# Joining the weights over the first two batches, with batch 0 in two visits, in a fused attention and MLP kernel

## The chip, the cores and the metric

The kernel runs on one core of one Trainium2 chip. The metric is the device time of one execution in microseconds (us). Three timed executions of the kernel before took 1055.58, 1061.92 and 1061.16 us, a median of 1061.16 us. A further execution was profiled.

## What is computed

A clustered attention feeds a mixing MLP. There are 4 batches, 8 heads, 768 positions and a head width of 64.

```python
q_assign = np.argmax(np.einsum('bhsd,hcd->bhsc', q_n, c_n), axis=-1)
k_assign = np.argmax(np.einsum('bhsd,hcd->bhsc', k_n, c_n), axis=-1)
mask = q_assign[:, :, :, None] == k_assign[:, :, None, :]
scores = np.where(mask, scale * np.matmul(q, k.transpose(0, 1, 3, 2)), -1000000000.0)
attn = softmax over the last axis
x = np.matmul(attn, v), heads side by side: (4, 768, 512)

h = x.transpose(0, 2, 1) @ U @ V          # mixing over the positions, rank 32
u = x + h.transpose(0, 2, 1)
out = u + np.maximum(u @ w_ch1, 0.0) @ w_ch2   # 512 -> 2048 -> 512
```

The weights of the MLP and of the mixing arrive as 64-bit floating-point numbers, seen as 64-bit integers.

## The kernel before

**Attention.** The 8 heads of a batch are taken in pairs, so there are 16 steps `i` ("head pairs"), four to a batch. A step loads queries and keys (`load`, tile `R`), rounds them to the upper part on ScalarE (`split_hi`, L390), subtracts for the lower part (`split_lo`, L395), assigns clusters, and places everything in rows of a large tile `arena` by DMA from the SP queue (`copy_rows`, L225; `place_clusters` copies the tile `ohT` there in four DMAs). `rowmax` multiplies keys by queries on TensorE (L455) and takes row maxima on VectorE (L457). `scores` (L493, L495) multiplies again with the maxima subtracted; ScalarE takes the exponential (L498, tile `pr`); GpSimd adds the tiles `pr` for the row sums (`weights`, L508); `values` multiplies by v (L516), ScalarE copies the result out (L520, twice in a step, once for each half). After the last step of a batch, `mix_u`, `mix_sum` and `mix_v` form `u`, and one DMA of 1536 KB writes it to memory (`u_scr`, L581).

**MLP.** `w_ch1` and `w_ch2` are cut into 8 tiles `k` of 256 hidden columns. A pair is one batch with one tile k; there are 32 pairs, in the order batch 0 with k 0 to 7, then batch 1, and so on. A pair makes seven products (a Strassen-like scheme: `product`, 42 matmuls, L687 to L689), into two buffers of PSUM named `ps_h`. The products' operands are sums of quarters of `u` (`split_u`, L633 and L634, seven a batch) and of a weight tile (`add_w` on GpSimd, L653, `split_w`, L660 and L662). VectorE combines the products (L697), ScalarE copies the first (L701, once a pair), takes the relu (L730), VectorE its lower part (`hl`, L727), and `gemm2` multiplies by the tile of `w_ch2` (36 matmuls, L740 to L742, operand split by `split_w2`, L671 on ScalarE and L669 on GpSimd). A batch's results stay in six accumulators `y` of PSUM until its last pair, where `finish` adds `u` (L749) and stores. The lower halves of a weight tile are subtracted on GpSimd in the first eight pairs and on VectorE afterwards (`split_w`).

**Joining.** A weight is turned from 64 to 32 bits in the kernel: half a tile (128 x 512) is loaded (`in_w`, 512 KB), ScalarE scales the upper words (L179), and three VectorE operations build the result (`join`, L189, L190, L192), which a DMA writes to `w_scr` (256 KB, L211). There are 32 half tiles. The first `EARLY` = 16 are joined during the attention, one every `PACE` = 6.5 units of the plan, with an intermediate in PSUM (`ps_t`). The other 16 come `LATE` = 1.985 units apart from the start of the MLP on, with the intermediate in SBUF (`rw_b`). Each tile is read again from `w_scr` when a pair uses it (`fetch_w`).

**Order.** Every step is put on one list with a planned time, by the tables `times`, `mixes`, `stages`, `mlp`, `order0` and `spots`. The list is sorted, and its order is the order of the instructions on each engine and in each queue; an engine waits at an instruction whose inputs aren't there. A step of the attention is 12 units of planned time, a pair of the MLP 7. `M0` is the unit at which the MLP starts. Planned times set order only, never a time of day.

**Where operands lie.** `operand` gives the 7 operand tiles of a batch places out of 9 in `arena`, in rotation, so two places of the next batch are free while a batch runs, and the others come free product by product in its last pair.

Of the kernel before, what the change touches and what calls it, by code (L numbers as in the profile page):

```python
# [45 lines left out]
P = 128  # L46
# [12 lines left out]
    "load0":          (-34.72, -34.25, -43.39,   None,   None,  -24.6),  # L59
    "load1":          (-26.03, -29.07, -30.74,   None,   None, -23.361),  # L60
    "sims":           ( -25.1, -28.59, -28.44,   None,   None, -21.52),
    "clusters_T":     (-19.416, -19.005, -18.681,   None, -13.278,  -13.9),
    "place_clusters": (-18.532, -16.49, -15.63,   None, -11.358, -12.11),
    "split_hi0":      (-29.17, -30.23, -24.29,   None,   None, -20.71),
    "split_lo0":      (-24.63, -24.44, -24.29,   None,   None, -18.43),
    "split_hi1":      (-23.89, -23.584, -24.34,   None,   None, -19.53),
# [876 lines left out]
```

## Time and profile before

| | |
|---|---|
| median of the timed executions | 1061.16 us |
| the profiled execution's own time | 1058.02 us |
| its span, first to last instruction | 1056.2 us |
| mean granted TensorE clock | 0.979 |
| busy: TensorE, VectorE, ScalarE, GpSimd | 93%, 67%, 42%, 56% |
| first product of the first pair | 503.4 us |

The attention fills the first 503 us of the span, the MLP the rest. A busy share is a mean over both; the prediction reads each part by itself. In rows of the timeline the first column is the start, the second the length, both in us; what stands in square brackets is how long the engine sat idle before that instruction, and what released it.

### The profile page before, as it was taken

The numbers are of one execution on the slowest core, as the hardware profiler recorded it, in microseconds if no ns is written. First come the engines' busy times: TensorE is split into PE (matmuls) and PEld (weight loads), VectorE is DVE, ScalarE is ACT, GpSimd is POOL, SyncE is SP. The second block draws the span as 40 slices with busy tenths as digits, with TensorE's granted clock in tenths as the row PEclk, the third lists the DMA queues.
The fourth block names the chain that finished last, engine by engine and source line by source line (L and its number), as shares of the span: only waits on it lengthen the run. The fifth ranks groups of instructions, "written<-read, shape, count | busy, mean of one in ns | idle before, by whom it ended". The sixth has DMA issues, their size and how long they took to land.

```text
span 1056.2 us, 14186 instructions
## 1 busy us (share of the span) xinstructions
PE 986.9 (93%) x5227; PEld 766.5 (73%) x5227; DVE 703.6 (67%) x1114; ACT 446.4 (42%) x633; POOL 590.3 (56%) x410
## 2 busy tenths in 40 slices
PE   6999999789998999998898898999999999999998
PEld 4666665565655676664677787888878888788887
DVE  5698777566876776646489867655486554865554
ACT  4454554345544556465233344223342234422321
POOL 4466676558756879766555667344373443734420
PEclk8899999899999999999999998999999999999999
DMA  6664564756547574600256751422115222152121
GB/s 164 172 149 121 145 173 102 232 143 162 162 106 225 157 190 107 200 1 25 99 183 204 240 195 44 169 79 101 70 71 178 80 102 70 71 179 76 44 101 60
DMA packets 43658, 135.99 MB, mean 129 GB/s; under 512 B 6539, under 2 KB 11141, under 8 KB 43077
## 3 DMA queue, kind: packets, MB, share of 16 engines
q1 hardware_dynamic: 43216, 135.00, 42.4%
q8 instruction: 41, 0.67, 0.3%
q14 instruction: 29, 0.23, 0.1%
q10 hardware_dynamic: 372, 0.10, 0.0%
HBM read 82.84 MB, written 20.97 MB: 98 GB/s over the span
## 4 chain that ended last, share of the span: by engine, by line
PE 62%; DVE 18%; DMA 7%; issue 4%; ACT 3%; POOL 3%; SPq 1%; ACTq 0%; DVEq 0%; POOLq 0%
PE o_ps L516 9%; PE y L741 6%; PE y L742 6%; PE y L740 6%; PE ps_h L687 6%; PE ps_h L688 6%; PE ps_h L689 6%; PE ps_max L455 5%; DMA rw<-in_w 4%; PE st L493 4%; PE st L495 4%; DVE m L457 3%; DVE arena L634 2%; DVE rw_t L192 2%; DVE hl L727 2%
## 5 line engine op out<-in xcount | busy, mean ns | idle before, releaser
L457 DVE TENSOR_REDUCE m<-ps_max 128x1 f32<-128x384 f32 x384 | 195.3, 548 | 108.9 <-PE ps_max L455 107.3
L508 POOL TENSOR_TENSOR T<-T,pr 128x768 f32<-128x768 f32 x120 | 227.8, 1898 | 60.3 <-ACT pr L498 36.5
L498 ACT ACTIVATE pr<-st 128x768 f32<-128x768 f32 x192 | 154.8, 811 | 84.2 <-PE st L495 68.9
L687 PE MATMUL ps_h<-arena,combos 128*128 128x384 f32 x448 | 154.2, 344 | 15.6 <-DVE c L697 15.0
L730 ACT ACTIVATE hh<-c 128x768 fp32r<-128x768 f32 x64 | 54.2, 846 | 243.6 <-DVE c L697 243.6
L742 PE MATMUL y<-w,hl 128*128 128x512 f32 x384 | 153.0, 399 | 1.8 <-DVE hl L727 1.7
L741 PE MATMUL y<-w,hh 128*128 128x512 f32 x384 | 153.9, 401 | 0.0
L740 PE MATMUL y<-w,hh 128*128 128x512 f32 x384 | 152.5, 397 | 0.0
L688 PE MATMUL ps_h<-arena,combos 128*128 128x384 f32 x448 | 151.5, 338 | 0.0
L689 PE MATMUL ps_h<-arena,combos 128*128 128x384 f32 x448 | 151.2, 338 | 0.0
L455 PE MATMUL ps_max<-arena 128*128 128x384 f32 x384 | 127.6, 385 | 19.8 <-DMA arena<-arena 4.3
L653 POOL TENSOR_TENSOR sums_w<-rw 128x256 f32<-128x256 f32 x64 | 52.6, 842 | 156.8 <-DVE combos L660 126.2
L516 PE MATMUL o_ps<-pr,vt 128*64 128x384 f32 x768 | 131.8, 492 | 6.8 <-ACT pr L498 6.0
L669 POOL TENSOR_TENSOR w<-w2f,w 128x1024 fp32r<-128x1024 f32 x32 | 78.3, 2447 | 77.3 <-ACT w L671 74.1
L455 PEld LDWEIGHTS ps_max<-arena 128*128 128x128 f32 x384 | 70.8, 196 | 60.7 <-issue 23.7
L727 DVE SCALAR_TENSOR_TENSOR hl<-c,hh 128x768 fp32r<-128x768 f32 x64 | 76.3, 1193 | 52.4 <-ACT hh L730 52.4
L493 PE MATMUL st<-arena 128*128 128x384 f32 x384 | 107.9, 363 | 0.9 <-ACT pr L498 0.7
L687 PEld LDWEIGHTS ps_h<-arena,combos 128*128 128x128 f32 x448 | 84.9, 190 | 32.5 <-DVE c L697 18.6
L508 POOL TENSOR_TENSOR T<-pr 128x768 f32<-128x768 f32 x30 | 57.0, 1899 | 87.0 <-ACT pr L498 86.8
L516 PEld LDWEIGHTS o_ps<-pr,vt 128*64 128x64 f32 x768 | 52.3, 137 | 73.1 <-issue 61.7
L495 PE MATMUL st<-arena 97*128 97x384 f32 x384 | 101.1, 345 | 1.4 <-DMA arena<-mT 1.4
L688 PEld LDWEIGHTS ps_h<-arena,combos 128*128 128x128 f32 x448 | 85.0, 190 | 7.6
(123 smaller groups left out, 1542.5 us busy)
## 6 DMA issues: line engine op xcount, KB each, us to landing
rw<-in_w SPq DMA_DIRECT2D x32, 512.0 KB
rw<-w_scr SPq DMA_DIRECT2D x32, 512.0 KB
w2f<-w_scr SPq DMA_DIRECT2D x32, 512.0 KB
R<-in_qk SPq DMA_DIRECT2D x32, 384.0 KB
arena<-arena SPq DMA_DIRECT2D x32, 384.0 KB
arena<-arena SPq DMA_DIRECT2D x64, 192.0 KB
u<-u_scr SPq DMA_DIRECT2D x16, 768.0 KB
w_scr<-rw_t SPq DMA_DIRECT2D x32, 256.0 KB
```

Source lines behind the costliest of these rows:

```text
L455: nc.tensor.matmul(ps[:, 0:HS], x1[:, 0, g // 2, g % 2, t * P:(t + 1) * P], x1[:, 1, h, g % 2, :], start=True, stop=True)
L457: nc.vector.reduce_max(live["m2", i][:, h, u:u + 1], ps[:, 0:HS], axis=AX.X)
L493: nc.tensor.matmul(st[:, j, 0:HS], x1[:, 1, hk, j, ks], x1[:, 0, h, j, :], start=True, stop=False)
L498: nc.scalar.activation(pr, st[:, :, 0:HS], AF.Exp, scale=SCALE)
L508: eng.tensor_add(T, live["p", i, h, 0] if c == 1 else T, live["p", i, h, c])
L516: nc.tensor.matmul(o_ps[64 * j:64 * j + 64, 0:HS], vv[:, c, j, :], pr[:, j, :], start=(c == 0), stop=(c == NT - 1))
L687: nc.tensor.matmul(ps, ah[:, d], oh[:, d], start=(d == 0), stop=False)
L688: nc.tensor.matmul(ps, ah[:, d], ol[:, d], start=False, stop=False)
L689: nc.tensor.matmul(ps, al[:, d], oh[:, d], start=False, stop=(d == 1))
L740: nc.tensor.matmul(y, hh[:, f, ts], w2[:, 0, f, :], start=(k == 0 and f == 0), stop=False)
L741: nc.tensor.matmul(y, hh[:, f, ts], w2[:, 1, f, :], start=False, stop=False)
L742: nc.tensor.matmul(y, hl[:, f, ts], w2[:, 0, f, :], start=False, stop=(k == NK - 1 and f == 1))
```

## The change

It has three parts.

1. **Joining spread.** 12 half tiles are joined during the attention, 9.53 units apart. The other 20 are joined in the first two batches of the MLP at the times in a new table `joins`, each relative to M0, by a new function `convert`: twelve of them build the weight tile in the place where its pair reads it, and write it to memory for later batches; eight (`STAGED`, half tiles 16 to 23) go through a tile `joined` to `w_scr`, as before. Each stage of `convert` (load, scale, join, store) has its offset in the row `late` of `stages`. The join's intermediate is the result tile itself, in SBUF. The sequence of the tiles (`blocks`) is written out.
2. **Another order of the pairs.** `runs` sets batch 0 with k 0 to 3, batch 1 with k 0 to 7, batch 0 with k 4 to 7, batch 2, batch 3. After the first visit `finish` adds the partial result to `u` and stores it to `u_scr`, from which the second visit fetches it. Batch 0 and batch 1 both keep their operands, in 14 places: 12 in `arena`, 2 in a new tile. Batch 1's operands are made in the pairs 2 to 4 (counted from 0), where they were made in the pairs 6 and 7. A second buffer `w2f_odd` takes the odd tiles of `w_ch2`. The lower halves of weight tiles are subtracted on GpSimd up to the pair 12.
3. **All tables of planned times are new**, with a table `lead` for the first six score tiles of step 0 and `paces` for the row maxima of the first steps.

```diff
 stages = {
-    "mix":  (  4.41,   7.02,  11.43,  15.04,  16.45,  17.16),
-    "w":    (36.161, 38.329, 40.954,  43.05),
-    "late": ( 9.201,   10.9,   11.5,   12.3),
+    "mix":  ( 4.442,  9.237, 21.481, 15.135, 28.889,  17.93),
+    "w":    ( 30.85, 37.709, 40.748, 43.339),
+    "late": ( -4.02, -1.242, -0.505,  0.183),
 }
-PACE, LATE, EARLY = 6.5, 1.985, 16
+PACE, EARLY = 9.53, 12
+STAGED = (16, 24)
+joins = [ 12.42, 18.256, 17.874, 23.279, 21.865, 30.275, 36.483, 42.327, 44.241, 48.068, 50.38, 53.5, 57.087, 57.953, 63.136, 62.997, 68.029, 70.82, 72.995, 78.476]
...
-    "place_clusters": (-18.532, -16.49, -15.63,   None, -11.358, -12.11),
+    "place_clusters": (-16.663, -19.154, -20.524,   None, -13.79, -13.047),
-    "rowmax":         (-14.88, -14.94,  -14.8, -12.18, -7.978, -10.78),
+    "rowmax":         (-14.783, -15.801, -17.043, -10.988, -8.892, -11.482),
...
+    runs = ((0, 0, 4), (1, 0, 8), (0, 4, 8), (2, 0, 8), (3, 0, 8))
+    pairs = [(r, b, k) for r, (b, k0, k1) in enumerate(runs) for k in range(k0, k1)]
...
     def operand(b, o):
-        s = (7 * b + order.index(o)) % 9
-        at = 0 if s == 8 else 2 * XS + 2 * HB * s
+        s = order.index(o) + (7 if b in (1, 2) else 0)
+        if s < 12:
+            at = 2 * HB * ((s + 4) % 12)
+            x = arena[:, at:at + 2 * HB]
+        else:
+            x = live["operands"][:, s - 12]
...
+    def convert(s, stage):
+        (k, m), half = blocks[s // 2], s % 2
+        cols = slice(512 * half, 512 * half + 512)
+        rw, g, joined = live["late_w"]
+        rw, g = rw[:, half], g[:, half]
+        direct = not STAGED[0] <= s < STAGED[1]
+        if stage == 0:
+            if half == 0 and direct:
+                live["f", k, m] = weight_tile(k, m)
+            nc.sync.dma_start(out=rw, in_=w[k, m, :, cols])
+        elif stage == 1:
+            nc.scalar.mul(g, words(rw)[1], 2.0 ** -112)
+        elif stage == 2:
+            t = (live["f", k, m][:, cols] if direct else joined).bitcast(I32)
+            merge(rw, g.bitcast(I32), t, t)
+        elif not direct:
+            nc.sync.dma_start(out=w_scr[k][m][:, cols], in_=joined)
+            stored.add((k, m, half))
+        elif half:
+            nc.sync.dma_start(out=w_scr[k][m], in_=live["f", k, m])
+            stored.update({(k, m, 0), (k, m, 1)})
...
-    def finish(b, j):
+    def finish(g, j):
+        r, b, k = pairs[g]
         h, t = divmod(j, HT)
-        u, y = live["u", b, h], live.pop(("y", b, j))
+        u, y = live["u", b, h], live.pop(("y", r, j))
         nc.vector.tensor_add(u[:, t, :], y, u[:, t, :])
-        nc.sync.dma_start(out=out[b, j * P:(j + 1) * P, :], in_=u[:, t, :])
+        if k == NK - 1:
+            nc.sync.dma_start(out=out[b, j * P:(j + 1) * P, :], in_=u[:, t, :])
+        elif t == HT - 1:
+            nc.sync.dma_start(out=u_scr[b][:, h * HT:(h + 1) * HT, :], in_=u)
...
-    for s in range(4 * NK):
+    for s in range(EARLY):
         for stage in range(4):
-            at(stages["w"][stage] + PACE * s if s < EARLY else M0 + stages["late"][stage] + LATE * (s - EARLY),
-               load_weights, s, stage)
+            at(stages["w"][stage] + PACE * s, load_weights, s, stage)
+    for s in range(EARLY, 4 * NK):
+        for stage in range(4):
+            at(M0 + joins[s - EARLY] + stages["late"][stage], convert, s, stage)
...
-            at(m + step, split_w, g, k // 2, k % 2 == 1)
+            at(m + step, split_w, pairs[g][2], nc.gpsimd if g < 13 else nc.vector, k // 2, k % 2 == 1)
```

Three places show how the order moves. The first is the SP queue around the store of batch 0's `u` (`u_scr`). Before:

```order
L581 DMA u_scr_102<-xt 128x3072
L171 DMA rw<-in_w 128x512
L211 DMA w_scr_1_87<-rw_t 128x512
L225 DMA arena<-arena 32x1536 x2
L225 DMA arena<-ohT 32x2x384 x4
```

Now (`L593` is the store, `L177` a load of half a weight tile):

```order
L177 DMA rw<-in_w 128x512
L237 DMA arena<-arena 64x1536 x2
L593 DMA u_scr_102<-xt 128x3072
L223 DMA w_scr_0_88<-rw_t 128x512
L237 DMA arena<-ohT 32x2x384 x4
L237 DMA arena<-arena 32x1536 x4
L347 DMA R<-in_qk 128x768 x2
L177 DMA rw<-in_w 128x512
```

The weight load that stood right behind the store stands eleven DMAs behind it, and the load ahead of the store has two copies between itself and the store.

The second place is VectorE in the joining part of the MLP, before in the pair 4 (`rw_b` and `rw_t` by L189 to L192 are joins, L697 combines products, L727 is the relu's lower part):

```order
L189 TENSOR_SCALAR rw_b<-rw_g 128x512
L190 SCALAR_TENSOR_TENSOR rw_b<-rw_g,rw_b 128x512
L192 SCALAR_TENSOR_TENSOR rw_t<-rw,rw_b 128x512
L697 TENSOR_TENSOR c_5718<-rw_t,ps_h 128x384
L727 SCALAR_TENSOR_TENSOR hl<-c_5718,hh 128x768
L697 TENSOR_TENSOR rw_t<-ps_h,rw_g 128x384
L697 TENSOR_TENSOR c_5810<-ps_h,rw_t 128x384
L189 TENSOR_SCALAR rw_b<-rw_g 128x512
L190 SCALAR_TENSOR_TENSOR rw_b<-rw_g,rw_b 128x512
L192 SCALAR_TENSOR_TENSOR rw_t<-rw,rw_b 128x512
L697 TENSOR_TENSOR c_5810<-ps_h,rw_t 128x384
```

Now, in the pairs 4 and 5 (`joined` by L194 to L197 is a join, L745 combines, L775 is the relu's lower part):

```order
L194 TENSOR_SCALAR joined<-late_g 128x512
L195 SCALAR_TENSOR_TENSOR joined<-late_g,joined 128x512
L197 SCALAR_TENSOR_TENSOR joined<-late_rw,joined 128x512
L745 TENSOR_TENSOR c_5820<-ps_h,rw_g 128x384
L745 TENSOR_TENSOR rw_g<-ps_h,rw_g 128x384
L745 TENSOR_TENSOR rw_t<-ps_h,rw_g 128x384
L745 TENSOR_TENSOR c_5820<-rw_t,ps_h 128x384
L775 SCALAR_TENSOR_TENSOR hl<-c_5820,hh 128x768
L745 TENSOR_TENSOR rw_t<-ps_h,rw_g 128x384
L745 TENSOR_TENSOR c_5898<-ps_h,rw_t 128x384 x2
```

Before, a join stood after every two or three combinations; now seven combinations and a lower part pass between this join and the next.

The third place is VectorE where batch 1's operands are made, in the pairs 3 and 4 (L686 is `split_u`, L798 is `finish`):

```order
L686 TENSOR_TENSOR arena<-turned,arena 128x768 x2
L775 SCALAR_TENSOR_TENSOR hl<-c_5618,hh 128x768
L798 TENSOR_TENSOR u<-y_5223,u 128x512
L745 TENSOR_TENSOR c_5678<-ps_h,rw_g 128x384
L798 TENSOR_TENSOR u<-y_5249,u 128x512
L686 TENSOR_TENSOR operands<-turned,operands 128x768
L194 TENSOR_SCALAR joined<-late_g 128x512
L195 SCALAR_TENSOR_TENSOR joined<-late_g,joined 128x512
L197 SCALAR_TENSOR_TENSOR joined<-late_rw,joined 128x512
L745 TENSOR_TENSOR rw_g<-ps_h,rw_g 128x384
```

Before, the same place (the pairs 6 and 7, `split_u` at L634) held no joins, and the six additions of `finish` followed it:

```order
L634 TENSOR_TENSOR arena<-turned,arena 128x768 x2
L697 TENSOR_TENSOR c_6201<-ps_h,rw_g 128x384
L634 TENSOR_TENSOR arena<-turned,arena 128x768
L697 TENSOR_TENSOR rw_g<-ps_h,rw_g 128x384
L660 TENSOR_TENSOR combos_107<-rw,combos_107 128x768
L634 TENSOR_TENSOR arena<-turned,arena 128x768
```

A batch's operands, the six additions and joins now meet in the same two pairs.

More of the change, by code (lines that the diff above doesn't have):

```diff
@@ L172, in fetch, with words, merge @@
         return rw
+    def words(rw):
+        w = rw.bitcast(I32).rearrange("p (n two) -> p n two", two=2)
+        return w[:, :, 0], w[:, :, 1].bitcast(F32)
     def upper(rw):
         r, n = rw.shape
-        g = home[0].tile([P, 512], F32, name="rw_g")[0:r, 0:n]
-        high = rw.bitcast(I32).rearrange("p (n two) -> p n two", two=2)[:, :, 1].bitcast(F32)
-        nc.scalar.mul(g, high, 2.0 ** -112)
-        return rw, g.bitcast(I32), None
-    def join(rw, g, t):
-        r, n = rw.shape
-        low = rw.bitcast(I32).rearrange("p (n two) -> p n two", two=2)[:, :, 0]
-        t = home[0].tile([P, 512], I32, name="rw_t")[0:r, 0:n]
-        b = (work("ps_t").bitcast(I32) if home[0] is raw else home[0].tile([P, 512], I32, name="rw_b"))[0:r, 0:n]
+        g = raw.tile([P, 512], F32, name="rw_g")[0:r, 0:n]
+        nc.scalar.mul(g, words(rw)[1], 2.0 ** -112)
+        return rw, g.bitcast(I32)
+    def merge(rw, g, b, t):
         nc.vector.tensor_scalar(b, g, 3, None, op0=ALU.logical_shift_left)
@@ L191, in join @@
                                        op0=ALU.bitwise_and, op1=ALU.bitwise_or)
-        nc.vector.scalar_tensor_tensor(out=t, in0=low, scalar=29, in1=b,
+        nc.vector.scalar_tensor_tensor(out=t, in0=words(rw)[0], scalar=29, in1=b,
                                        op0=ALU.logical_shift_right, op1=ALU.bitwise_or)
-        return rw, g, t
+    def join(rw, g):
+        r, n = rw.shape
+        t = raw.tile([P, 512], I32, name="rw_t")[0:r, 0:n]
+        merge(rw, g, work("ps_t").bitcast(I32)[0:r, 0:n], t)
+        return t.bitcast(F32)
     parts, stored = {}, set()
-    blocks = sorted(((k, m) for k in range(NK) for m in range(2)), key=lambda x: (x[0] + x[1], -x[1]))
+    blocks = ((0, 0), (1, 0), (0, 1), (2, 0), (1, 1), (3, 0), (2, 1), (3, 1),
+              (4, 0), (5, 0), (4, 1), (5, 1), (6, 0), (7, 0), (6, 1), (7, 1))
     def load_weights(s, stage):
@@ L678, in product @@
     def product(g, p):
-        b, k = divmod(g, NK)
+        _, b, k = pairs[g]
         a, o = products[p]
@@ L814, in clustered_attention_moe @@
             h, c = divmod(k, NT)
[L815 removed]
+            at(when("scores", i) + (lead[k] if i == 0 and k < GV else k), scores, i, h, c)
             at(when("values", i) + GV * (k // GV) + GV - 1 + 0.001 * (k % GV), values, i, h, c)
@@ L860, in splits, with fetches @@
             at(m + step, fn, *args)
-    ng = B * NK
-    at(t_w0, fetch_w, 0, 0)
+    def fetches(time, g, m):
+        k = pairs[g][2]
+        s = 2 * blocks.index((k, m))
+        if s < EARLY or STAGED[0] <= s < STAGED[1] or any(x[2] == k for x in pairs[:g]):
+            at(time, fetch_w, k, m)
+    ng = len(pairs)
+    fetches(t_w0, 0, 0)
     weights_of(0, t_sums)
-    at(t_w1, fetch_w, 1, 0)
-    at(t_w2, fetch_w, 0, 1)
+    fetches(t_w1, 1, 0)
+    fetches(t_w2, 0, 1)
     for h in range(2):
@@ L874, in clustered_attention_moe @@
     for g in range(ng):
-        b, k = divmod(g, NK)
+        r, b, k = pairs[g]
         m = M0 + 7 * g
```

176 lines of the change are left out of this document (91 added, 85 removed).

## The prediction

> **What bounds the kernel now.** I read the page first: the busy shares, then the strip of 40 slices.
>
> ```profile
> PE 986.9 (93%) x5227; PEld 766.5 (73%) x5227; DVE 703.6 (67%) x1114; ACT 446.4 (42%) x633; POOL 590.3 (56%) x410
> PE   6999999789998999998898898999999999999998
> PEclk8899999899999999999999998999999999999999
> ```
>
> TensorE is the bound, and the change takes none of its matmuls away. A gain can only come from its idle time and from stretches at a lower granted clock. Next came the windows of the two stages (columns: length; busy us of TensorE, of its weight loads, VectorE, ScalarE, GpSimd; clock; DMA share; GB/s).
>
> ```profile
> 503.00:1056.00 553.00, 530.00 (x2601) 463.06 (x2597) 349.16 (x440) 190.30 (x254) 251.27 (x182) 0.99 0.33 115
> 0.00:503.00 503.00, 456.85 (x2630) 303.47 (x2630) 354.44 (x674) 256.06 (x379) 339.02 (x229) 0.97 0.54 144
> ```
>
> The attention leaves 503 - 457 = 46 us idle and loses about 3% of 503 = 15 us to the clock. The MLP leaves 23 us and loses about 5. Both are spread, so I looked for repeated work that should take equal times.
>
> In the attention, ScalarE copies the result of each half step. These are the ends of steps 2, 10, 11 and 12.
>
> ```profile
> 125.89 0.48 ACT L520 COPY os<-o_ps 128x384 f32<-128x384 f32 x1 [3.16 <-PE o_ps L516]
> ...
> 369.61 0.48 ACT L520 COPY os<-o_ps 128x384 f32<-128x384 f32 x1 [2.79 <-PE o_ps L516]
> ...
> 394.12 0.48 ACT L520 COPY os<-o_ps 128x384 f32<-128x384 f32 x1 [2.86 <-PE o_ps L516]
> ...
> 423.44 0.48 ACT L520 COPY os<-o_ps 128x384 f32<-128x384 f32 x1 [2.55 <-PE o_ps L516]
> ```
>
> Step 11 took 24.5 us, step 12, with the mixing of a batch inside, 29.3. Neither holds a join. Steps 3 to 10, six plain and two with mixing, would take 6 x 24.5 + 2 x 29.3 = 205.6 us at that pace; they took 243.7. So 38 us are lost where the joins are.
>
> In the MLP, ScalarE copies the first product once a pair. These are pairs 1, 8, 9, 14 and 16.
>
> ```profile
> 519.97 0.48 ACT L701 COPY rw_g<-ps_h 128x384 f32<-128x384 f32 x1 [1.87 <-PE ps_h L689]
> ...
> 657.39 0.48 ACT L701 COPY rw_g<-ps_h 128x384 f32<-128x384 f32 x1 [0.65 <-PE ps_h L689]
> 673.06 0.48 ACT L701 COPY rw_g<-ps_h 128x384 f32<-128x384 f32 x1 [0.77 <-PE ps_h L689]
> ...
> 751.35 0.48 ACT L701 COPY rw_g<-ps_h 128x384 f32<-128x384 f32 x1 [1.00 <-PE ps_h L689]
> ...
> 789.71 0.46 ACT L701 COPY rw_g<-ps_h 128x384 f32<-128x384 f32 x1
> ```
>
> A clean pair takes 15.67 us. A switch of batches without joins (pairs 14 to 16) costs 38.36 - 2 x 15.67 = 7.0 us over that. From pair 1 to pair 8 it is 137.4 us for seven pairs and one switch: 137.4 - 109.7 - 7.0 = 20.7 us are lost while 16 joins run.
>
> **The change, part by part.** The sum is made against the profiled execution's 1058.0 us (span 1056.2); it lies 3.1 us under the median of 1061.2.
>
> *1. The hole behind the store of batch 0's u.*
>
> ```profile
> 183.91 1.78 SPq L581 DMA_DIRECT2D u_scr<-xt  x1
> 185.75 0.43 SPq L171 DMA_DIRECT2D rw<-in_w  x1
> 197.28 0.66 ACT L179 ACTIVATE rw_g<-rw 128x512 f32<-128x512 f32 x1 [10.19 <-DMA rw<-in_w]
> 190.00:195.00 5.00, 3.59 (x22) 1.35 (x20) 1.02 (x2) 0.00 (x0) 2.10 (x2) 1.00 0.96 362
> 195.00:200.00 5.00, 0.43 (x2) 0.30 (x4) 0.00 (x0) 2.72 (x4) 0.34 (x1) 0.88 0.05 12
> 200.00:205.00 5.00, 5.00 (x17) 3.86 (x14) 3.15 (x6) 2.24 (x4) 1.51 (x2) 0.50 0.81 186
> ```
>
> The weight load is queued right behind 1536 KB. ScalarE stands at the join's scaling for 10.2 us with exponentials behind it, TensorE idles 1.41 + 4.57 = 6.0 us and then runs 5 us at half clock, 2.5 us more. The change issues each weight load 6.86 units ahead of its scaling (37.709 - 30.85), where it was 2.17; at 24.5 / 12 = 2.04 us a unit that is 14 us against 4.4, and the order shows this load ahead of the store. I take -8 us, between -9 and 0 (another load in the same place). What could be late next is the copies of `ohT`, which now come two places behind the store.
>
> *2. Four joins fewer in the attention.*
>
> ```profile
> L190 DVE SCALAR_TENSOR_TENSOR ps_t<-rw_g,ps_t 128x512 int32<-128x512 int32 (+2 forms) x19 | 12.6, 664 | 0.7
> L192 DVE SCALAR_TENSOR_TENSOR rw_t<-rw,ps_t 128x512 int32<-128x512 int32 (+2 forms) x19 | 12.4, 655 | 0.7
> L189 DVE TENSOR_SCALAR ps_t<-rw_g 128x512 int32<-128x512 int32 (+2 forms) x19 | 12.4, 652 | 0.0
> ```
>
> One costs VectorE 0.65 + 0.66 + 0.66 = 1.97 us and holds one of four PSUM buffers. Four make 7.9 us. VectorE isn't full in this stage (354 of 503), so not all of it is on the path: between 0 and -8, I take -3, nearer to the end where it hides. The 12 that stay are also further apart (9.53 units against 6.5); that is in item 3.
>
> *3. The other tables of the attention.* Of the 38 us, items 1 and 2 take 11; 27 are left in steps 3 to 10, and the start and the end have holes of their own. A table's worth can't be read from its numbers. The longer leads speak for a gain: `load0` of a usual step stands 11.1 units ahead of its rounding (-40.53, -29.39), where it was 5.6. One lead is shorter (the second rival). I take -5, between -25 and +15.
>
> *4. Joins thinned in the MLP.*
>
> ```profile
> L189 DVE TENSOR_SCALAR rw_b<-rw_g 128x512 int32<-128x512 int32 x16 | 14.8, 925 | 1.9 <-ACT rw_g L179 1.7
> L190 DVE SCALAR_TENSOR_TENSOR rw_b<-rw_g,rw_b 128x512 int32<-128x512 int32 x16 | 15.9, 996 | 0.5
> L192 DVE SCALAR_TENSOR_TENSOR rw_t<-rw,rw_b 128x512 int32<-128x512 int32 x16 | 18.5, 1159 | 0.5
> L727 DVE SCALAR_TENSOR_TENSOR hl<-c,hh 128x768 fp32r<-128x768 f32 x12 | 18.4, 1531 | 6.4 <-ACT hh L730 6.4
> L697 DVE TENSOR_TENSOR rw_t<-ps_h,rw_g 128x384 f32<-128x384 f32 x11 | 6.1, 552 | 3.1 <-PE ps_h L689 2.9
> ```
>
> Here a join costs 3.08 us. A pair without joins needs 2 x 1.53 + 7 x 0.55 = 6.9 us of VectorE. In pairs 2 to 6 the order has 3 joins a pair: 6.9 + 9.2 = 16.1 of 15.67 us, more than there is, and TensorE must wait. In the new order pairs 5 to 10 have 2 or 3, mostly 2: 13.1 of 15.67. Pair 2 has four (19.2 us), so some 4 us stay there. Thirteen joins' worth of lesser collisions at perhaps 0.4 us make 5 more; that is an estimate between nothing and the 1.3 us a join that the 20.7 us show now. So 9 to 10 of the 20.7 us stay: -11, between -21 and +5.
>
> *5. Batch 1's operands among the joins.* Seven subtractions and six additions of `finish` in the pairs 3 and 4:
>
> ```profile
> L634 DVE TENSOR_TENSOR arena<-turned,arena 128x768 fp32r<-128x768 f32 x28 | 42.1, 1512 | 13.0 <-ACT arena L633 12.9
> L749 DVE TENSOR_TENSOR u<-y,u 128x512 f32<-128x512 f32 x24 | 16.4, 686 | 5.9 <-PE y L742 5.9
> ```
>
> 7 x 1.51 + 6 x 0.69 = 14.7 us beside 2 x 6.9 and two joins, 6.2: 34.7 us in two pairs and a switch, 31.3 + 7.0. It fits barely. At pairs 6 and 7 the same work without joins already made a hole (640 to 645, below). I take +2, between 0 and +6.
>
> *6. One more switch of batches.* Pair 12 needs no new operands. Six additions, 4.1 us of VectorE, go beside pairs that have no joins any more; two stores and two loads go on the SP queue. +1, between 0 and +3.
>
> *7. The later switches.* Seven of 14 places are free for the next batch, where two of nine were. Of the 7.0 us, 24 transposes are work (some 4 us); the rest is waiting. Twice -1: -2, between -5 and 0.
>
> Sum: -8 - 3 - 5 - 11 + 2 + 1 - 2 = -26. From 1058.0 that is 1032, from the median 1035; I say 1033.
>
> A rule weighs against items 4 and 5, and these rows show its effect.
>
> ```profile
> 548.31 0.42 DVE L189 TENSOR_SCALAR rw_b<-rw_g 128x512 int32<-128x512 int32 x1
> 555.43 2.41 DVE L189 TENSOR_SCALAR rw_b<-rw_g 128x512 int32<-128x512 int32 x1
> 555.18 2.39 POOL L660 TENSOR_TENSOR combos<-sums_w,combos 128x1024 fp32r<-128x1024 f32 x1 [3.48 <-ACT combos L662]
> 555.00:560.00 5.00, 1.91 (x10) 1.36 (x8) 4.93 (x6) 0.10 (x1) 3.84 (x3) 1.00 0.46 173
> 560.00:565.00 5.00, 4.66 (x16) 4.19 (x17) 4.00 (x6) 2.48 (x5) 1.82 (x3) 0.66 0.81 262
> ```
>
> The same operation took 0.42 us, and 2.41 while a GpSimd operation ran; it ended 0.3 us after that one, and TensorE idled 3.1 us and then had clock 0.66. The Trainium skill ("SBUF — State Buffer", Who interferes with whom) says that the two engines share a port pair that one holds for a whole instruction while the other is blocked. The trace agrees. By that rule alone the three operations of a join could each wait out one GpSimd operation. The change keeps GpSimd at its subtractions for the pairs 8 to 12 too, so all 20 joins run beside it. That gives the first rival.
>
> **The rivals.**
>
> *Joins as dear as now.* If what a join costs TensorE is its wait for GpSimd and not the crowding, 20 joins cost 20 x 1.3 = 26 us instead of the 10 in my sum: +16, 1048. For it: the row at 555.43. Against: in the window 535 to 640 VectorE's joins stand so close that any delay lands on a product.
>
> *Cluster rows late.* In a usual step (nine of sixteen) `place_clusters` stands at -16.66 and the first row maximum at -14.78 + 0.39: 2.3 units or 4.6 us, where it was 3.9 units or 8.0.
>
> ```profile
> 434.87 2.69 SPq L225 DMA_DIRECT2D arena<-ohT  x4
> 436.95 5.85 DMA arena<-ohT
> 640.00:645.00 5.00, 1.97 (x7) 1.54 (x6) 3.72 (x5) 3.98 (x5) 4.92 (x4) 0.76 0.01 3
> ```
>
> From the first issue to the landing it took 436.95 + 5.85 - 434.87 = 7.9 us. Covered before by 8.0, it would be short by 3.3 us in nine steps, and a hole of that size brings a lower clock (0.66 after 3.1 us idle), 1.7 us each: 9 x 5.0 = 45, so 1077, slower. It decides if the SP queue reaches these copies only at their planned place. Against it: the queue runs ahead of the other engines where nothing holds it, and the tile copied is made no later than before. The Trainium skill ("TensorE: Matmul & The Clock Gate", Part 1) puts the clock's window at about 3.4 us; by it such a hole could also cost nothing more than itself. That would be 9 x 3.3 = 30 us and 1062.
>
> *The tables find most of the 27 us.* Item 3 at -25 gives 1012. For it: step 11 shows that a step can run in 24.5 us. Against: that step holds no join, and twelve joins stay.
>
> That the change doesn't thin the joins can be left out: the order shows it.
>
> **How the numbers follow.** My forecast, items near their chosen values, has a chance of 0.60, with 1018 to 1045 as its own range. Joins as dear as now: 0.18. Most of the 27 us found: 0.10. Cluster rows late, in whole or in good part: 0.12. A range of 1008 to 1056 holds the first and nearly all of the next two, and leaves out the late cluster rows and some tail, about 0.17. One per cent, which is about what can be told from no change here, puts the bounds at 1050.5 and 1071.8. Faster: 0.60, 0.10, and of the dear joins 0.08, together 0.78. Within 1%: 0.10 of the dear joins and 0.02 of late rows, 0.12. Slower: 0.10.
>
> **What would show it.** Item 1: no ScalarE wait of 10 us for `in_w`, and no slice at 0.5 clock near 200 us. Items 2 and 3: the first product starts at about 488 us instead of 503 or 504. Item 4: pairs 5 to 11 at 16 to 16.5 us. Item 5: a hole in pairs 2 to 4. The first rival would show in pairs of 17 us or more up to pair 11; the second in waits of `rowmax` for `ohT`. I am wrong if the attention is longer than 503 us, or the first half of the MLP isn't shorter.

## The result, and the profile after

The changed kernel takes 1031.1 us (median of 4 runs, 1029.85 to 1033.91) beside 1059.45 us of the kernel before on the same chip (4 runs). The ratio is 0.974 with a 95% interval of 0.970 to 0.978. 1033 us were forecast. The profiled execution is the longest of the four, 1033.9 us with a span of 1032.1; the span before was 1056.2, so 24.1 us went.

The page of the changed kernel, busy shares and two lines of the strip of 40 slices (25.8 us each):

```profile
PE 979.0 (95%) x5227; PEld 764.5 (74%) x5227; DVE 715.4 (69%) x1110; ACT 443.1 (43%) x633; POOL 622.8 (60%) x420
...
PE   7999999999999999989978999899989999899998
PEclk8999999999999999999998999999999999999999
```

The low slices in the middle are now the one from 439 us on, lightly, and those from 516 to 568 us: pairs 2 to 4 of the MLP.

Its windows, the MLP from 470 us on and the attention ahead of it (length; TensorE, weight loads, VectorE, ScalarE, GpSimd; clock; DMA share; GB/s):

```profile
470.00:1032.00 562.00, 530.57 (x2607) 463.99 (x2605) 363.22 (x449) 191.27 (x259) 282.90 (x192) 0.99 0.34 119
0.00:470.00 470.00, 448.40 (x2623) 300.50 (x2623) 352.16 (x662) 251.87 (x374) 339.87 (x228) 0.99 0.54 147
```

The attention is 33 us shorter: its idle time on TensorE fell from 46 to 21.6 us, and TensorE's busy time from 456.9 to 448.4, at a granted clock of 0.99 instead of 0.97. The MLP became longer, 562 us instead of 553, with 31.4 us idle instead of 23. So the total is where the forecast put it, and its parts are not.

ScalarE's copies at the ends of steps 2, 10, 11 and 12, to set beside those of before:

```profile
121.62 0.48 ACT L532 COPY os<-o_ps 128x384 f32<-128x384 f32 x1 [3.16 <-PE o_ps L528]
...
339.15 0.48 ACT L532 COPY os<-o_ps 128x384 f32<-128x384 f32 x1 [3.53 <-PE o_ps L528]
...
364.73 0.48 ACT L532 COPY os<-o_ps 128x384 f32<-128x384 f32 x1 [3.58 <-PE o_ps L528]
...
394.54 0.48 ACT L532 COPY os<-o_ps 128x384 f32<-128x384 f32 x1 [4.15 <-PE o_ps L528]
```

Steps 3 to 10 take 339.15 - 121.62 = 217.5 us, where they took 243.7; step 11 takes 25.6 and step 12 29.8, about as long as before (24.5 and 29.3). The gain lies in the steps with the joins, as it should if the loss of 38 us there was real. The windows of these eight steps, before and now, show what went:

```profile
125.89:369.61 243.72, 221.35 (x1272) 146.18 (x1273) 174.36 (x335) 122.90 (x178) 164.14 (x88) 0.97 0.59 162
121.62:339.15 217.53, 212.88 (x1275) 142.86 (x1276) 166.70 (x323) 119.90 (x174) 166.49 (x90) 1.00 0.60 167
```

TensorE's idle time fell from 22.4 to 4.7 us, and its busy time by 8.5 us at the higher clock.

The copies of the first product of pairs 0, 1, 3, 4, 5, 6, 11 and 31 in the MLP:

```profile
471.31 0.48 ACT L749 COPY rw_g<-ps_h 128x384 f32<-128x384 f32 x1 [0.75 <-PE ps_h L737]
...
490.98 0.48 ACT L749 COPY rw_g<-ps_h 128x384 f32<-128x384 f32 x1 [4.16 <-PE ps_h L737]
...
527.41 0.46 ACT L749 COPY rw_g<-ps_h 128x384 f32<-128x384 f32 x1
550.59 0.47 ACT L749 COPY rw_g<-ps_h 128x384 f32<-128x384 f32 x1
573.21 0.48 ACT L749 COPY rw_g<-ps_h 128x384 f32<-128x384 f32 x1 [0.55 <-PE ps_h L737]
588.89 0.48 ACT L749 COPY rw_g<-ps_h 128x384 f32<-128x384 f32 x1 [0.98 <-PE ps_h L737]
...
676.27 0.48 ACT L749 COPY rw_g<-ps_h 128x384 f32<-128x384 f32 x1
...
1005.43 0.48 ACT L749 COPY rw_g<-ps_h 128x384 f32<-128x384 f32 x1 [0.99 <-PE ps_h L737]
```

The first copy stands at 471.3 instead of 504.8 (-33.5). From pair 0 to pair 31 it is 534.1 us instead of 526.2 (+7.9); after the last copy come 26.7 us instead of 25.3 (+1.4). Pairs 3 and 4 take 23.2 and 22.6 us where a clean pair takes 15.67. This is the hole at pair 4, on VectorE, on GpSimd and on TensorE:

```profile
554.53 2.82 DVE L686 TENSOR_TENSOR operands<-turned,operands 128x768 fp32r<-128x768 f32 x1
557.27 2.06 DVE L194 TENSOR_SCALAR joined<-late_g 128x512 int32<-128x512 int32 x1
559.36 2.71 DVE L195 SCALAR_TENSOR_TENSOR joined<-late_g,joined 128x512 int32<-128x512 int32 x1
562.10 1.09 DVE L197 SCALAR_TENSOR_TENSOR joined<-late_rw,joined 128x512 int32<-128x512 int32 x1
```

```profile
554.12 2.41 POOL L708 TENSOR_TENSOR combos<-sums_w,combos 128x1024 fp32r<-128x1024 f32 x1 [3.04 <-ACT combos L710]
556.49 2.55 POOL L708 TENSOR_TENSOR combos<-rw,combos 128x768 fp32r<-128x768 f32 x1
559.00 2.52 POOL L717 TENSOR_TENSOR w<-w2f,w 128x1024 fp32r<-128x1024 f32 x1
561.48 2.30 POOL L701 TENSOR_TENSOR sums_w<-rw 128x256 f32<-128x256 f32 x2
```

```profile
563.72 0.69 PE L735 MATMUL ps_h<-arena,combos 128*128 128x384 f32 x1 [4.96 <-DVE rw_g L745]
```

VectorE's first three operations each end 0.3 to 0.8 us behind one of GpSimd's; the join needs 5.9 us, and TensorE has by then waited 5 us for the combining addition queued behind it.

### The profile page after: what moved, and what is told of

It is laid out like the page before. It is cut to its first block, busy times and chain, and to the rows that moved or that the text cites. A ratio compares the mean times of both kernels' runs of the same rounds, so it can differ in the third digit from the quotient of the medians.

```text
span 1032.1 us, 14214 instructions
## 1 busy us (share of the span) xinstructions
PE 979.0 (95%) x5227; PEld 764.5 (74%) x5227; DVE 715.4 (69%) x1110; ACT 443.1 (43%) x633; POOL 622.8 (60%) x420
## 4 chain that ended last, share of the span: by engine, by line
PE 72%; DVE 19%; issue 3%; ACT 3%; DMA 1%; POOL 1%; ACTq 0%; SPq 0%; DVEq 0%; POOLq 0%
PE o_ps L528 11%; PE ps_max L467 7%; PE y L789 7%; PE y L790 7%; PE y L788 7%; PE ps_h L735 6%; PE ps_h L736 6%; PE ps_h L737 6%; PE st L505 5%; PE st L507 5%; DVE m L469 2%; DVE hl L775 2%; DVE combos L708 2%; DVE arena L686 2%; DVE c L745 1%
## 5 line engine op out<-in xcount | busy, mean ns | idle before, releaser
L735 PE MATMUL ps_h<-arena,combos 128*128 128x384 f32 x384 | 133.0, 346 | 22.4 <-DVE rw_g L745 11.7
L467 PE MATMUL ps_max<-arena 128*128 128x384 f32 x384 | 124.0, 379 | 9.3 <-ACT ohT L394 2.0
L736 PE MATMUL ps_h<-arena,combos 128*128 128x384 f32 x384 | 130.5, 340 | 0.0
L737 PE MATMUL ps_h<-arena,combos 128*128 128x384 f32 x384 | 130.1, 339 | 0.0
L505 PE MATMUL st<-arena 128*128 128x384 f32 x384 | 104.2, 353 | 3.0 <-ACT pr L510 3.0
L775 DVE SCALAR_TENSOR_TENSOR hl<-c,hh 128x768 fp32r<-128x768 f32 x64 | 80.9, 1264 | 30.9 <-ACT hh L778 30.9
L735 PEld LDWEIGHTS ps_h<-arena,combos 128*128 128x128 f32 x384 | 72.8, 190 | 39.3 <-DVE rw_g L745 13.4
L701 POOL TENSOR_TENSOR sums_w<-rw 128x256 f32<-128x256 f32 x64 | 58.9, 939 | 50.2 <-DVE combos L708 50.2
L717 POOL TENSOR_TENSOR w<-w2f,w 128x1024 fp32r<-128x1024 f32 x16 | 39.7, 2479 | 80.3 <-ACT w L719 80.3
L790 PEld LDWEIGHTS y<-w,hl 128*128 128x128 f32 x384 | 72.7, 189 | 16.6
```

The source lines that it names most:

```text
L467: nc.tensor.matmul(ps[:, 0:HS], x1[:, 0, g // 2, g % 2, t * P:(t + 1) * P], x1[:, 1, h, g % 2, :], start=True, stop=True)
L505: nc.tensor.matmul(st[:, j, 0:HS], x1[:, 1, hk, j, ks], x1[:, 0, h, j, :], start=True, stop=False)
L735: nc.tensor.matmul(ps, ah[:, d], oh[:, d], start=(d == 0), stop=False)
L736: nc.tensor.matmul(ps, ah[:, d], ol[:, d], start=False, stop=False)
L737: nc.tensor.matmul(ps, al[:, d], oh[:, d], start=False, stop=(d == 1))
L790: nc.tensor.matmul(y, hl[:, f, ts], w2[:, 0, f, :], start=False, stop=(g in lasts and f == 1))
```

## The experiments

All twelve are read by the same marks: the ratio to the kernel before, the copy of the first product (end of the attention), steps 3 to 10, and pair 0 to pair 31. Profiles of kernels that agree up to there put the end of step 2 anywhere from 119.6 to 121.8 us, and kernels with the same attention put steps 3 to 10 anywhere from 215.1 to 217.5, so a single mark is good to some 2 us. Each ratio is to runs of the kernel before made beside that kernel, whose medians lie between 1055.5 and 1059.5 us; so ratios are compared, not medians.

| kernel | median us | ratio (95%) | first copy | steps 3-10 | pairs 0-31 |
|---|---|---|---|---|---|
| before | 1059.5 | 1 | 504.8 | 243.7 | 526.2 |
| changed | 1031.1 | 0.974 (0.970-0.978) | 471.3 | 217.5 | 534.1 |
| sixteen early | 1034.2 | 0.979 (0.975-0.984) | 479.5 | 215.9 | 526.0 |
| all early | 1047.8 | 0.993 (0.990-0.995) | 507.0 | 241.2 | 511.3 |
| attention tables alone | 1035.9 | 0.981 (0.975-0.986) | 476.2 | 225.2 | 536.2 |
| load lead alone | 1062.2 | 1.006 (1.004-1.009) | 511.7 | 249.4 | 524.8 |
| no late join operations | 1006.7 | 0.954 (0.951-0.957) | 468.0 | 216.1 | 509.7 |
| low parts on ScalarE | 1021.5 | 0.968 (0.965-0.972) | 469.7 | 217.2 | 520.8 |
| early joins in place | 1071.7 | 1.015 (1.012-1.019) | 508.2 | 243.2 | 533.1 |
| sixteen early, mended | 1029.5 | 0.975 (0.971-0.979) | 470.5 | 215.1 | 527.3 |
| low parts on VectorE | 1032.6 | 0.976 (0.973-0.979) | 475.0 | 215.8 | 532.1 |
| both of these | 1034.4 | 0.977 (0.973-0.980) | 479.6 | 216.5 | 526.3 |
| DMA rows alone | 1062.6 | 1.004 (1.001-1.006) | 510.6 | 248.9 | 523.8 |
| no early join operations | 1025.7 | 0.969 (0.964-0.973) | 465.0 | 211.2 | 533.9 |

Three of them leave work out and measure its price alone: the two without join operations, and the one with the low parts on ScalarE, which copies where the kernel subtracts.

**Where do the 33 us of the attention come from?** First the tables without the rest: the kernel before with `times`, `mixes`, `order0`, `lead`, `paces`, `spots`, the row "mix" and the MLP's opening from the changed kernel.

```
 stages "w":   (36.161, 38.329, 40.954,  43.05)      kept
 PACE, LATE, EARLY = 6.5, 1.985, 16                  kept
-times, mixes, order0, spots, "mix", "open", "fetch_u0", "turn_u0", "split0", "first", "second"  (before)
+times, mixes, order0, spots, lead, paces, "mix", "open", ... (changed kernel)
```

> The kernel before with the placing tables of the attention and of the MLP's opening from the changed kernel; the 16 joins of the attention keep their own places (6.5 units apart, the load 2.2 units ahead of the scaling), and the MLP keeps its order of pairs and its 16 joins in pairs 1 to 8. Theory A (the tables carry the gain): the first copy between 471 and 480 us instead of 504.8, total 1026 to 1035. Theory B (fewer joins and their spacing carry it): the first copy at 490 us or later, total 1044 or more.

The first copy came at 476.2: 28.6 of the 33.5 us are the tables', and in steps 3 to 10 18.5 of the 26.2 us. The total gained less, because the MLP of before behind the new opening lost 10 us. The DMA queue shows what went with the tables. Before, the store of u was issued at 183.91, and ScalarE waited 10 us for the weight load behind it. Here, in the timeline of the SP queue and of ScalarE:

```profile
173.62 0.33 SPq L585 DMA_DIRECT2D u_scr<-xt  x1
174.00 0.44 SPq L175 DMA_DIRECT2D rw<-in_w  x1
...
181.71 0.67 ACT L183 ACTIVATE rw_g<-rw 128x512 f32<-128x512 f32 x1
```

The load stands right behind the store as it did, with its short lead, and is scaled without a wait: the queue reached the store 10 us earlier, while step 4 ended only 5.5 us earlier (174.7 against 180.2). Then the lead alone, and the DMA issues of a usual step alone, both in the kernel before:

```
-    "w":    (36.161, 38.329, 40.954,  43.05),
+    "w":    ( 30.85, 37.709, 40.748, 43.339),
```

> The kernel before with one row of numbers changed: the weight loads of the attention are issued 6.9 units ahead of their scaling instead of 2.2. Item 1 of the prediction alone: 8 us less, total 1050 to 1053, and no 10 us ScalarE wait for in_w near 187 to 197 us. Rival (the hole moves to whatever stands behind the store next): the same total within 2 us. If the short lead cost time in all 16 joins and not only behind the store: 15 us or more, total below 1045.

```
 "most" column only:
-load0 -34.72   load1 -26.03   place_keys_hi -20.566  place_keys_lo -20.062  place_queries -16.28   place_ones -14.55   load_v -19.692
+load0 -40.531  load1 -29.642  place_keys_hi -23.83   place_keys_lo -19.187  place_queries -17.815  place_ones -19.506  load_v -14.291
```

> The kernel before with only the places of seven operations of a usual step from the changed kernel, all of them DMA issues: load0, load1, place_keys_hi, place_keys_lo, place_queries, place_ones and load_v. If the order on the DMA queues makes the gain of the attention's tables: steps 3 to 10 at 225 to 233 us instead of 243.7, no 10 us wait for in_w, total 1040 to 1048. If the places of the computing steps make it, or only all of them together: 240 us or more, total 1053 or more.

Both were slightly slower than before, by 0.6% and 0.4%, and steps 3 to 10 by 5.7 and 5.2 us. With the lead the 10 us wait of ScalarE did go, as item 1 said, but TensorE was idle for 24.9 us in these steps, where it had been 22.4, and its clock was 0.96 instead of 0.97. Its first three waits there (waiter, releaser, us in total, times, longest):

```profile
PE ps_max L455 <- DMA arena<-arena: 5.3, 2, 2.6
PE ps_max L455 <- DVE rw_t L192: 4.5, 5, 1.6
PE st L495 <- DMA arena<-mT: 2.8, 2, 2.3
```

With the DMA rows ScalarE still waited for `in_w`, 11.1 us in four waits, the longest 8.4. So neither part of the tables carries the gain alone. The tables as a whole do, and which of their numbers are needed was not found.

**What does a join cost in the attention?** Four joins more, at the changed kernel's spacing:

```
-PACE, EARLY = 9.53, 12
+PACE, EARLY = 9.53, 16
-joins = [ 12.42, 18.256, 17.874, 23.279, 21.865, ...
+joins = [ 21.865, ...
```

> The changed kernel with 16 joins in the attention again instead of 12 (at the same spacing of 9.53 units); the four joins that leave the MLP are those of pairs 1 to 3. Theory A (the attention's gain of 33 us comes from its tables, and a join there hides at 0.8 us or less; in the MLP a join costs TensorE 1.1 us, and the holes between 534 and 565 us are those of the four early joins): the first product's copy moves from 471.3 to 472 to 474.5 us, pair 0 to pair 31 shortens from 534.1 by 4 to 8 us, total 1024 to 1030. Theory B (a good part of the 33 us comes from the four joins that left the attention, 2 us each or more): the copy at 479 us or later, total 1033 or more. Theory C (the MLP's loss is the early switch and batch 1's operands, not the joins): the copy as in A, the MLP unchanged within 2 us, total 1032 to 1034.

The first copy came 8.1 us later, as the second theory had it, but nearly all of it in one step: step 13 took 37.3 us instead of 30.0. The waits of the SP queue there, and its issues:

```profile
SPq L177 <- DVE rw_t L197: 11.0, 1, 11.0
```

```profile
415.50 0.34 SPq L177 DMA_DIRECT2D rw<-in_w  x1
415.88 0.43 SPq L666 DMA_DIRECT2D u<-u_scr  x1
```

The weight load stood 11 us at the head of the queue until a join freed a raw tile (the MLP's first weight tile held the other), and the second half of u, which TensorE's transposes wait for, stood behind it. So the two weight tiles of the MLP were fetched later, and the last four weight loads too:

```
-    "open":     ( 0.339,  8.397, -53.59, -24.403,  1.634, -27.049),
+    "open":     ( 0.339,  8.397,    -33,      -8,  1.634, -27.049),
-            at(stages["w"][stage] + PACE * s, load_weights, s, stage)
+            at(stages["w"][stage] + PACE * s + (2.15 if s >= 12 and not stage else 0), load_weights, s, stage)
```

> 16 joins in the attention as in the run with sixteen, but the two weight tiles of the MLP are fetched later (33 and 8 units ahead of its start instead of 53.6 and 24.4) and the last four weight loads 2.15 units later, so that no load stands on the SP queue waiting for a raw tile with the loads of u behind it. If that queue made the 37.3 us of step 13: steps 12 and 13 at 30 us again, first copy at 471 to 474, MLP 526 as there, total 1024 to 1028. If the four joins themselves cost 2 us each: first copy at 478 us or later, total as there, 1032 or more.

Step 13 fell to 32.3 us and the first copy to 470.5. Steps 12 to 15 are 3.0 us longer than in the changed kernel, 0.75 us a join, while the MLP is 6.8 us shorter, 1.7 us a join. The ratio of 0.975 can't be told from the 0.974 of the changed kernel. Next, all 32 joins in the attention:

```
-    "w":    ( 30.85, 37.709, 40.748, 43.339),
+    "w":    (  34.5, 37.709,   40.2,   42.5),
-PACE, EARLY = 9.53, 12
+PACE, EARLY = 4.4, 32
-joins = [ 12.42, ...
+joins = []
```

> The changed kernel with all 32 joins in the attention (spacing 4.4 units) and none in the MLP; the order of the pairs stays. Theory A: 20 more joins cost the attention 0.5 to 1 us each, the first copy at 481 to 491 us; the MLP loses the joins' 21 us, pair 0 to pair 31 at 511 to 515 us; total 1020 to 1031. Theory B: 2 us or more a join, the first copy at 511 us or later, total 1048 or more. Theory C: the MLP keeps most of its loss beside the switches, 525 us or more, because the new order of the pairs and the operands of batch 1 cause it; total 1042 or more.

20 joins more, with their loads, scalings and stores, cost the attention 35.7 us, 1.8 us each, between the two theories. The MLP without joins takes 511.3 us, as theory A had it. Last, the 12 early joins without their VectorE operations:

```
-            parts["w", s] = join(*parts["w", s])
+            parts["w", s] = parts["w", s][1].bitcast(F32)
```

> The changed kernel with the three VectorE operations of the 12 early weight joins left out (the scaled upper words are stored in their place, so those blocks are wrong); loads, scalings and stores stay. If a join's VectorE time is on the path in the attention, as 1.8 us for each of the 20 joins added in the run with all 32 says: steps 3 to 10, with 10 joins, at 200 to 208 us instead of 217.5. If 12 joins hide where they stand now, and only more of them cost: 213 us or more.

Steps 3 to 10 fell by 6.3 us to 211.2, or by 3.9 from the shortest that the same attention took elsewhere: 0.4 to 0.6 us for each of ten joins. This lies between the two expectations, nearer to the second. So a join costs 0.4 to 0.8 us where twelve or sixteen stand, and 1.8 us where 32 do; what raises it isn't shown.

**What does a join cost in the MLP, and why?** The 20 late joins without their VectorE operations:

```
-            nc.scalar.mul(g, words(rw)[1], 2.0 ** -112)
+            nc.scalar.mul(live["f", k, m][:, cols] if direct else joined, words(rw)[1], 2.0 ** -112)
         elif stage == 2:
-            merge(rw, g.bitcast(I32), t, t)
+            pass
```

> The changed kernel with the three VectorE operations of the 20 late joins left out (ScalarE's scaling writes straight into the target tile, so those blocks of the weights are wrong); their loads, scalings and stores stay. With all 32 joins in the attention the MLP took 511.3 us from pair 0 to pair 31, with 20 late joins 534.1. If the whole price of a late join is its VectorE time: 510 to 515 us, total 1008 to 1013, first copy unchanged at 471. If loads, scalings and the one buffer for late joins carry part of it: 520 us or more, total above 1017.

509.7 us: the VectorE operations are the whole price, 24.4 us or 1.2 us for each join. Pairs 0 to 12, which hold all of the joins, in the changed kernel and in this run:

```profile
471.31:708.32 237.01, 216.88 (x1042) 186.20 (x1042) 169.91 (x208) 84.22 (x117) 146.58 (x97) 0.97 0.44 150
468.01:680.71 212.70, 210.10 (x1042) 183.60 (x1042) 102.89 (x148) 84.42 (x116) 142.25 (x97) 0.99 0.48 167
```

Of the 24.3 us between them, 17.5 are idle time of TensorE, and 6.8 are busy time at the lower clock. In the changed kernel these products wait for VectorE's combining additions, and for no operand that GpSimd makes; without the join operations the longest such wait is 0.3 us. Their two largest waits in pairs 0 to 12 of the changed kernel:

```profile
PE ps_h L735 <- DVE rw_g L745: 11.7, 4, 5.0
PE ps_h L735 <- DVE c L745: 5.3, 6, 2.5
```

Now GpSimd is relieved in the pairs with joins, and nothing added to VectorE; where GpSimd subtracted, ScalarE copies:

```
         if low:
-            eng.tensor_sub(lo, x, hi)
+            if eng is nc.gpsimd:
+                nc.scalar.copy(lo, x)
+            else:
+                eng.tensor_sub(lo, x, hi)
```

> The changed kernel with GpSimd's two subtractions of split_w in the first 13 pairs replaced by ScalarE copies of the same tiles (the low parts are then wrong): GpSimd loses about 4.5 us a pair, ScalarE gains 1.9. If late joins cost what they wait for GpSimd: the three operations of a join fall from 3.4 us to 2 us or less, and pair 0 to pair 31 takes 514 to 524 us instead of 534.1. If crowding of VectorE or the wait for ScalarE sets the price: 530 us or more.

The MLP fell by 13.4 us. VectorE's time in the middle operation of the 20 joins, in the changed kernel (from the windows with that line alone; length, VectorE's busy time, clock, DMA share, GB/s):

```profile
470.00:720.00 250.00, 27.10 (x20) 0.97 0.45 154
```

and in this run:

```profile
470.00:720.00 250.00, 17.06 (x20) 0.99 0.46 158
```

All three operations together fell from 67.4 to 54.3 us, 3.37 to 2.71 us a join, where 2 us or less was expected. Other operations of VectorE became shorter too: `hl` fell from 1.30 to 1.12 us. So a good half of the 24.4 us went with GpSimd's two subtractions, and 11 us stayed. To relieve GpSimd and still subtract, the two operations go to VectorE:

```
-            at(m + step, split_w, pairs[g][2], nc.gpsimd if g < 13 else nc.vector, k // 2, k % 2 == 1)
+            at(m + step, split_w, pairs[g][2], nc.vector, k // 2, k % 2 == 1)
```

> The changed kernel with split_w's two low parts on VectorE in all pairs, not only from pair 13 on (in the later pairs they take 1.27 and 1.37 us there). GpSimd loses 4.5 us a pair, VectorE gains 2.6. If late joins cost what they wait for GpSimd (the run with these parts on ScalarE: 520.8 us from pair 0 to pair 31): 520 to 530 us, total 1017 to 1027. If VectorE is then too full in the pairs with joins (6.9 + 2.6 + 2 x 2.5 = 14.5 of 15.67 us, 19.5 in the pair with four): 534 us or more, total 1031 or more.

> The last two taken together: 16 joins in the attention with the later fetches of the weight tiles (first copy at 470.5, pairs 527.3), and split_w's low parts on VectorE in all pairs. If both gains add: first copy at 470 to 473, pair 0 to pair 31 at 514 to 522 us, total 1012 to 1021, the fastest of all. If the joins of pairs 1 to 3 were what waited for GpSimd, only one of the gains is left: 1022 to 1028.

Neither gained. The MLP fell by 2.0 us only: the joins went to 2.58 us each, but 24 subtractions took their place on VectorE (35 us between 476 and 692 us). And step 14 took 28.5 us instead of 22.2, because the change also put pair 0's subtractions, which run in the attention, on VectorE:

```profile
423.24 2.74 DVE L708 TENSOR_TENSOR combos<-sums_w,combos 128x1024 fp32r<-128x1024 f32 x1
425.90 2.55 DVE L708 TENSOR_TENSOR combos<-rw,combos 128x768 fp32r<-128x768 f32 x1
```

and the window there, with TensorE busy for 1.62 of 5 us:

```profile
425.00:430.00 5.00, 1.62 (x8) 1.04 (x5) 5.00 (x6) 0.70 (x2) 4.92 (x2) 0.78 0.12 26
```

That part of the loss isn't the joins'; a version that leaves pair 0 on GpSimd was not tried.

**The PSUM buffer of an early join.** The prediction held the PSUM buffer against a join of the attention. Here it is taken away, and the join is made in its SBUF target like the late ones:

```
-        merge(rw, g, work("ps_t").bitcast(I32)[0:r, 0:n], t)
+        merge(rw, g, t, t)
```

> The changed kernel with the 12 joins of the attention made in their SBUF target, as the late ones are, instead of over a PSUM buffer of the four that the products share. If the buffer is what a join costs there: the waits of the row maximum's products for rw_t go, steps 3 to 10 shorten from 217.5 us by 2 to 6 us. If VectorE's time is: no gain, and where the operations then wait for GpSimd they grow from 0.65 to some 1 us each, steps 3 to 10 at 217 to 223 us.

Both theories were far off: steps 3 to 10 became 25.7 us longer. (The three joins of the mixing's weights share the function and moved too; they lie ahead of step 3.) The three operations in the attention of the changed kernel,

```profile
L195 DVE SCALAR_TENSOR_TENSOR ps_t<-rw_g,ps_t 128x512 int32<-128x512 int32 x12 | 8.3, 696 | 0.4
L197 DVE SCALAR_TENSOR_TENSOR rw_t<-rw,ps_t 128x512 int32<-128x512 int32 x12 | 8.2, 686 | 0.4
L194 DVE TENSOR_SCALAR ps_t<-rw_g 128x512 int32<-128x512 int32 x12 | 8.2, 684 | 0.0
```

in this run,

```profile
L195 DVE SCALAR_TENSOR_TENSOR rw_t<-rw_g,rw_t 128x512 int32<-128x512 int32 x12 | 23.4, 1951 | 0.4
L197 DVE SCALAR_TENSOR_TENSOR rw_t<-rw,rw_t 128x512 int32<-128x512 int32 x12 | 20.3, 1694 | 0.4
L194 DVE TENSOR_SCALAR rw_t<-rw_g 128x512 int32<-128x512 int32 x12 | 11.9, 988 | 0.0
```

and, from its timeline, one of the joins with the GpSimd operations beside it and the product that waits:

```profile
204.22 0.41 DVE L194 TENSOR_SCALAR rw_t<-rw_g 128x512 int32<-128x512 int32 x1
204.66 2.21 DVE L195 SCALAR_TENSOR_TENSOR rw_t<-rw_g,rw_t 128x512 int32<-128x512 int32 x1
206.90 2.17 DVE L197 SCALAR_TENSOR_TENSOR rw_t<-rw,rw_t 128x512 int32<-128x512 int32 x1
...
204.23 6.52 POOL L520 TENSOR_TENSOR T<-T,pr 128x768 f32<-128x768 f32 x3
...
209.60 1.15 PE L467 MATMUL ps_max<-arena 128*128 128x384 f32 x2 [3.93 <-DVE m L469]
```

GpSimd adds back to back, 6.52 / 3 = 2.17 us each, and each of the two operations with two SBUF inputs takes as long as one of these. With one input in PSUM none of them in steps 3 to 10 of the changed kernel took more than 0.70 us, with GpSimd busy for 166 of these 217.5 us. The Trainium skill ("SBUF — State Buffer", Who interferes with whom) states just this: a VectorE instruction with at most one SBUF input, outside the two-port modes, does not contend with GpSimd, and one with two SBUF inputs contends with a GpSimd instruction that reads SBUF. The trace agrees (0.70 against 1.95 us). The prediction took the page's lock for any of the three operations and drew no difference between the joins of the two stages. What the buffer alone costs this run can't tell; in steps 3 to 10 of the changed kernel TensorE's row maxima waited 0.6 us in all for a join.

## Why the prediction was right

The total was right and its split was not: two misses of the sum cancelled, and that they did is luck. The span went by -33.5 (attention) + 7.9 (MLP) + 1.4 (tail); the sum had -16 for items 1 to 3 and -10 for items 4 to 7. So the attention came out 17.5 us better than the sum, and the rest 19 us worse; items 3 and 4 lie near opposite ends of their own ranges.

*Item 1* (-8): the hole went. Step 5, which held it, takes 28.0 us instead of 37.7; in steps 3 to 10 no wait of ScalarE is longer than 4.1 us; and in the old hole's window TensorE is busy at full clock:

```profile
195.00:200.00 5.00, 4.74 (x27) 3.11 (x29) 4.46 (x11) 3.33 (x5) 4.84 (x3) 1.00 0.15 54
```

The reason given for it failed. The load's lead of 6.86 units, where it was 2.17, was neither enough (alone, steps 3 to 10 grew by 5.7 us) nor needed (with the old lead and the new tables there is no hole).

*Item 2* (-3): confirmed in size. Four joins measured 3.0 us in steps 12 to 15, and ten 3.9 to 6.3.

*Item 3* (-5, from -25 to +15): the step that failed most. The attention less item 2 gained some 30 us, where items 1 and 3 had 13. The tables alone give 28.6 with the hole's end included; some 2 us are left for the wider spacing and the longer lead together. The prediction said that "a table's worth can't be read from its numbers", and then took a value near nothing; the 27 us that it had counted as lost in those steps were the better guide. So the third rival's item came true. The 38 us "lost where the joins are" need not be the joins': in the changed kernel the same steps shorten by 6.3 us at most when the joins' operations are left out.

*Item 4* (-11): failed. The joins cost 22.9 us in the MLP (534.1 - 511.3), or 24.4 by the run without their operations, not 9 to 10. The step that fell is "lesser collisions at perhaps 0.4 us": it is 1.2 us a join in the mean, near the 1.3 of before. The count of VectorE's time per pair (13.1 of 15.67 us) took averages. In the trace half of the 20 joins run through in 1.9 us; the other ten take 3.4 to 7.6 us, and a product waits behind such a one, as in the hole at pair 4. The count was off as well: by the copies of the first product, pair 2 holds two joins and pair 8 four, where it gave four to pair 2. Those of pairs 1 to 3 are the dearest, 1.7 to 2 us each (6.8 to 8.1 us for four); the other sixteen still cost 1.0 to 1.1. So the first rival's term came true as well (20 x 1.3 = 26), without its total, since item 3 paid for it. Its cause, the wait for GpSimd, is shown for a good half of the price (13.4 of 24.4 us).

*Items 5 to 7* (+1 together): by the run with all joins early, the MLP beside its joins is 511.3 us, where before it was 526.2 - 20.7 = 505.5: +5.8. The opening, for which the sum had no term, took +3; the two later switches cost 1.0 to 1.4 us more each instead of 1 less; the early switch with batch 1's operands is as cheap as a switch was (6 us against 7), so items 5 and 6, taken without joins beside them, were too dear by some 3 us. Why the later switches became dearer isn't shown.

*Cluster rows late*: did not happen. TensorE's waits in steps 3 to 10 of the changed kernel, the first two (waiter, releaser, us in total, times, longest):

```profile
PE st L507 <- DMA arena<-mT: 1.6, 2, 0.8
PE ps_max L467 <- ACT ohT L394: 1.0, 1, 1.0
```

No wait for the copies of `ohT` among them; the one microsecond is for the tile itself.

Of the marks named beforehand, item 1's came, the first product came 18 us earlier than said, the holes in pairs 2 to 4 came, and "pairs 5 to 11 at 16 to 16.5 us" is missed by a little: they run from 15.7 to 18.9, 17.2 in the mean of pairs 5 to 10. "The first half of the MLP isn't shorter", which was to prove the forecast wrong, did come (291.4 us from pair 0 to pair 16, where it was 284.9); the total was right all the same.

## What to carry to other kernels

Where repeated steps take longer than their clean length, the excess is a first estimate of what a better placing can give; here 26 of 38 us came, 18.5 of them from tables of which the two parts tried alone lost time. Before work is moved to another stage, its price there is measured by leaving its operations out: here a join cost 0.4 to 0.8 us in the attention and 1.2 in the MLP, so moving four of them one way or the other hardly mattered. In the run with sixteen early joins one issue that waited 11 us for a free tile held back the load behind it on its DMA queue; the queue's own list of waits named it.

## What the runs showed of the hardware

A VectorE operation on two SBUF inputs took 1.95 us in the mean beside busy GpSimd, and 0.70 with one of them in PSUM, although undisturbed (0.41 us for the one-input form in SBUF, 0.68 into PSUM) PSUM is not the faster place. In steps 3 to 10, ten joins moved from PSUM to SBUF added 25.7 us, at least four times what their operations had cost there (6.3 us at most by the run without them); the first product came 37 us later, with the mixing's three joins moved too. Part of that is the clock: in steps 3 to 10 the granted clock fell from 1.00 to 0.95, and TensorE's busy time for the same 1275 products rose from 212.9 to 222.3 us, beside 16 us more of idle time.
